# An attention and mixture-of-experts kernel: the first expert's load and making unpinned and in order of use, one cast two steps later

## The chip, the cores and the metric

The kernel runs on one core of a Trainium2 chip. The core has a matrix engine (TensorE, PE in the profile; its weight loads are shown apart as PEld), VectorE (DVE), ScalarE (ACT), GpSimd (POOL) and SyncE (SP), which here only issues DMAs. Each engine carries out its own instructions strictly in the order in which they stand in its queue, and waits for others by semaphores. Matmuls write to PSUM, everything else lies in SBUF, and 16 DMA engines move data between SBUF and the chip's memory. The metric is the time of one execution in microseconds; smaller is better.

## The reference

Clustered attention is followed by a mixture of eight experts. Batch B is 4, 8 heads, 768 tokens of 64 numbers; the experts see 3072 tokens of 512 numbers.

```python
mask = q_assign[:, :, :, None] == k_assign[:, :, None, :]
scores = np.where(mask, scale * q @ k.T, -1e9)
x = softmax(scores) @ v                      # (3072, 512) after reordering
P = np.exp(x @ w_gate - max)
for _ in range(8):                           # balance rows and columns
    P /= P.sum(1); P /= P.sum(0); P *= N / E
for e in range(8):
    h = np.maximum(x @ w1[e], 0.0)           # 512 -> 1024
    out += P[:, e:e + 1] * (h @ w2[e])       # 1024 -> 512
```

## The kernel before

**Two stages.** The attention stage is written as small processes (load a pair of heads, split it, chunk of exponentials, values, norms and so on) that a planner in the kernel, `Planner.run`, puts into one order by costs and due times. `Planner.keep_order` then pins that order: each new instruction gets a dependency, without a semaphore, on the instruction before it on its engine, so that the scheduler of the language, which would otherwise choose among what is ready, keeps it. The expert stage follows; its order is written out by hand, as generators that are advanced step by step, and `keep_order` is called after each step, so it is pinned too. `self.last` holds the last instruction of each engine and `self.traced` how many have been pinned; because both simply go on from attention to the experts, the first instruction of the expert stage on each engine is pinned behind the last one of attention on that engine, on SP too.

**An iteration.** The expert stage takes a batch b (768 tokens, `xs[b]`, seven combinations of its four quarters) and a piece of an expert: 256 of its 1024 hidden columns, four pieces an expert, numbered `idx`. `layer1` forms the hidden block from seven products of quarter blocks in place of eight (the names A11 to S4 are the seven combinations of the weights' quarters, B11 to T4 those of x). Every operand is a high and a low float16 part, so a product is three matmuls on each of two column blocks. The seven products, each followed by a `yield`, are the seven steps m = 0 to 6 of an iteration; their order of use is A11, S2, A12, S3, S1, A22, S4. They use two PSUM banks (`h_ps`). `layer2` multiplies by the second matrix and runs one iteration later, one token tile a step (`before`). At each step other work is advanced beside it: the balancing of the gates (`gates`, L1023 to L1052, on DVE with small matmuls on PE), the scan of the next expert's weights for its largest value (`scan`, L286), the loading, maximum and splitting of the next batch's x (`next_x`, loads at L1152, maxima at L286, splits at L300 and L303), and the making of the next piece (`making`).

**Making a piece.** `load_raw` brings a piece of w1 (`r1`) and of w2 (`r2`) by the DMAs at L1074 and L1078. The raw tiles are two, used in turn (`wp0`, `wp1`). `make_w` scales both (L1087, L1098), forms the four sums S1 to S4 (L1096), casts the seven blocks to a high float16 part on ACT (L1101, L1104) and subtracts it for the low part (L1102, L1105), into the tile `wa`; then it does the same with w2 into `wb` (L1107, L1108). The casts are on ACT, the sums and subtractions on POOL, but for piece 0, which is made by DVE, all at once, ahead of the loop over the iterations. In the loop one part of the making is done in each of the steps m = 0 to 4, the cast and subtraction of `wb` in the fifth. In the iterations of an even batch (b = 0) the made piece is stored to memory (`store_w`, L1113 and L1114, on SP at the iteration's start), whence the other batches load it.

**Memory.** Attention's tile pools are closed when it ends, and the expert stage's pools are placed in the same part of SBUF in the order of the code. An instruction that writes to an expert tile therefore waits until those attention tiles are no longer read that lay there.

**Around the change.** After `plan.run()` the code goes `load_raw(0)`, `load_raw(1)`, `make_w(0, wt, nc.vector)` to its end, and then the loop. The first iteration puts on SP the store of piece 0, `load_raw(2)`, two scan tiles and the four quarters of batch 1's x. Just before all of these, the end of attention has the last store of x (`xd<-xT`, L918), which waits for the last multiplication of attention's output by its row factors (L909). The logits for the gates come from the same x (L935 to L951).

Of the kernel before, what the change touches and what calls it, by code (L numbers as in the profile page):

```python
# [13 lines left out]
AF = mybir.ActivationFunctionType  # L14
ALU = mybir.AluOpType
# [5 lines left out]
P = 128  # L21
# [37 lines left out]
class Planner:  # L59
# [16 lines left out]
    def keep_order(self):  # L76

        for i in self.instructions()[self.traced :]:
            if i.engine in self.last:
                info = mybir.DependencyInfo(mybir.DependencyClass.NoSync, mybir.DependencyReason.DATA)  # L80
                self.tc.add_manual_dep(i, self.last[i.engine], info, reason="planned order")
            self.last[i.engine] = i.name
        self.traced = len(self.instructions())

    def copied(self, time):

        self.queues = max(self.queues, self.now.time + 0.55) + time
        return self.queues + 1.4
# [64 lines left out]
def attn_moe_kernel(  # L153
# [11 lines left out]
    nc = tc.nc  # L165
# [50 lines left out]
    KC = NC // 2  # L216
# [10 lines left out]
    s1 = const.tile([P, E], F32, name="s1")  # L227
    s2 = const.tile([P, E], F32, name="s2")
# [79 lines left out]
    with ExitStack() as actx:  # L308
# [104 lines left out]
        plan = Planner(tc)  # L413
# [641 lines left out]
    A22, A11, A12, S1, S2, S3, S4 = range(7)  # L1055

    def w_tiles(made):

        pool = wq0 if made else wq1
        wa = pool.tile([P, 2, 7, KC, P], F16, name="wa", bufs=3 if made else 2)  # L1060
        wb = pool.tile([P, 2, 2, DO], F16, name="wb")
        return wa, wb
# [4 lines left out]
    raws = {}  # L1067
# [13 lines left out]
    def make_w(idx, wt, by=nc.gpsimd):  # L1081

        e = idx // NP2
        r1, r2 = raws.pop(idx)
        wa, wb = wt
        raw = r1[:, 0 : 4 * KC * P]
        nc.scalar.activation(raw, raw, AF.Copy, scale=s1[:, e : e + 1])  # L1087
        A = raw.rearrange("p (k c t f) -> p t k c f", k=2, c=KC, t=2)
        S_ = r1[:, 4 * KC * P :].rearrange("p (o c f) -> p o c f", o=4, c=KC)
        for o, a, b_, op in (  # L1090
            (0, A[:, 0, 0], A[:, 0, 1], ALU.add),
            (1, S_[:, 0], A[:, 1, 0], ALU.subtract),
            (2, A[:, 1, 0], A[:, 0, 0], ALU.subtract),
            (3, A[:, 1, 1], S_[:, 1], ALU.subtract),
        ):
            by.tensor_tensor(out=S_[:, o], in0=a, in1=b_, op=op)  # L1096
        yield
        nc.scalar.activation(r2, r2, AF.Copy, scale=s2[:, e : e + 1])  # L1098
        yield
        for o, a in ((A22, A[:, 0, 1]), (slice(A11, A12 + 1), A[:, 1])):  # L1100
            nc.scalar.copy(wa[:, 0, o], a)  # L1101
            by.tensor_tensor(out=wa[:, 1, o], in0=a, in1=wa[:, 0, o], op=ALU.subtract)  # L1102
        yield
        nc.scalar.copy(wa[:, 0, 3:7], S_)  # L1104
        by.tensor_tensor(out=wa[:, 1, 3:7], in0=S_, in1=wa[:, 0, 3:7], op=ALU.subtract)  # L1105
        yield
        nc.scalar.copy(wb[:, 0], r2)  # L1107
        by.tensor_tensor(out=wb[:, 1], in0=r2, in1=wb[:, 0], op=ALU.subtract)  # L1108
        yield

    def store_w(idx, wt):
        fa, fb = flat(*wt)
        nc.sync.dma_start(out=wd[idx][:, 0:W1C], in_=fa)  # L1113
        nc.sync.dma_start(out=wd[idx][:, W1C:], in_=fb)  # L1114
# [185 lines left out]
    load_raw(0)  # L1300
    load_raw(1)
    wt = made[0] = w_tiles(True)
    for _ in make_w(0, wt, nc.vector):
        pass
    t = 0
    for n, (b, e) in enumerate(order):
        if e == 0:
# [4 lines left out]
        for f2 in range(NP2):  # L1312
# [5 lines left out]
            if t in begins:  # L1318
                i = begins[t]
                made[i] = w_tiles(True)  # L1320
                making = make_w(i, made[i])
                if i + 1 < NI:
                    load_raw(i + 1)
# [33 lines left out]
            if nb is not None:  # L1357
                wt = made.pop(nidx) if nb == 0 else wn
# [27 lines left out]
```

## Time and profile before

| what | value |
|---|---|
| median of 3 runs | 2471.73 us (2467.83 to 2471.76) |
| the profiled execution | 2472.1 us, span 2470.3 us |
| PE busy | 2380.3 us, 96% of the span |
| DVE, ACT, POOL busy | 1360.9, 834.8 and 668.6 us |
| DMA | 320.29 MB, mean 130 GB/s |
| mean granted PE clock | 0.990 of full speed |

Times in the profile are counted from the start of the span. A row of the timeline gives start, duration, engine, line, operation, output and inputs; in brackets the idle time of the engine before it and what ended it. SPq is SP's queue of DMA issues: its rows show when a DMA is issued, not when the data have landed. A row of the waits gives who waited for whom, the total, the number of times and the longest. Rows that gather a line's instructions give the shortest, median and longest duration in ns and the first and last start.

### The profile page before, as it was taken

How to read it: one execution, taken by the hardware profiler on the slowest of the kernel's cores; microseconds unless marked ns; L12 is line 12 of the kernel's file. 1: busy time of each engine (PE TensorE's matmuls, PEld its weight loads, DVE VectorE, ACT ScalarE, POOL GpSimd, SP SyncE). 2: the span in 40 equal slices, each digit the busy share in tenths (PEclk: the TensorE clock that was granted, in tenths of full speed). 3: DMA queues.
4: the chain of work that ended last, by engine and by line, in shares of the span. 5: the costliest groups of instructions: out<-in, count | busy, mean ns of one | idle time of the engine just before them, and what ended most of it. 6: DMA issues, size and time to landing. Idle time of an engine off the chain costs nothing.

```text
span 2470.3 us, 32700 instructions
## 1 busy us (share of the span) xinstructions
PE 2380.3 (96%) x12848; PEld 1274.8 (52%) x12848; DVE 1360.9 (55%) x2372; ACT 834.8 (34%) x1608; POOL 668.6 (27%) x712
## 2 busy tenths in 40 slices
PE   7999999966999999999999999999999999999999
PEld 4555655533545555555555555555555555555554
DVE  7888888847555454545454445544444444444444
ACT  4555555543243333333333323222121222122121
POOL 5776777734053333222222221000000000000000
PEclk9999999988999999999999999999999999999999
DMA  6545465243356353536352334222322222222322
GB/s 145 117 104 117 106 151 137 72 171 134 122 212 240 148 185 139 198 128 218 114 211 105 134 133 157 95 94 95 113 98 94 94 106 106 94 95 99 113 103 90
DMA packets 154681, 320.29 MB, mean 130 GB/s; under 512 B 61088, under 2 KB 90528, under 8 KB 154016
## 3 DMA queue, kind: packets, MB, share of 16 engines
q1 hardware_dynamic: 154528, 318.21, 39.2%
q8 instruction: 101, 1.65, 0.3%
q14 instruction: 52, 0.43, 0.1%
HBM read 230.74 MB, written 58.72 MB: 117 GB/s over the span
## 4 chain that ended last, share of the span: by engine, by line
PE 87%; DVE 8%; ACT 2%; DMA 1%; issue 1%; POOL 1%; SPq 0%; ACTq 0%; DVEq 0%; POOLq 0%
PE h_ps L1181 34%; PE o_ps L1251 13%; PE o_ps L1249 13%; PE o_ps L1250 13%; PE av_ps L820 4%; PE max_ps L693 3%; PE exp_ps L761 2%; PE exp_ps L762 2%; DVE mrt L697 2%; DVE hl L1197 1%; PE misc_ps L553 1%; DVE vsum L503 1%; POOL psum L787 0%; DVE am L286 0%; ACT pe L768 0%
## 5 line engine op out<-in xcount | busy, mean ns | idle before, releaser
L1181 PEld LDWEIGHTS <-wa 128*128 128x128 f16 x5376 | 527.0, 98 | 454.5 <-issue 22.0
L1181 PE MATMUL h_ps<-xsT,wa 128*128 128x384 f16 x3072 | 584.7, 327 | 9.5 <-DVE gm L240 4.8
L1251 PE MATMUL o_ps<-wb,hl 128*128 128x512 f16 x1536 | 584.4, 380 | 8.9 <-DVE hl L1197 8.9
L1197 DVE SCALAR_TENSOR_TENSOR hl<-c,hh 128x384 f16<-128x384 f32 x512 | 312.0, 609 | 509.5 <-ACT hh L1194 509.3
L1250 PE MATMUL o_ps<-wb,hh 128*128 128x512 f16 x1536 | 584.4, 380 | 0.0
L1249 PE MATMUL o_ps<-wb,hh 128*128 128x512 f16 x1536 | 584.3, 380 | 0.0
L1194 ACT ACTIVATE hh<-c 128x384 f16<-128x384 f32 x512 | 267.6, 523 | 921.8 <-DVE c L1209 914.2
L1181 PE MATMUL h_ps<-xsB,wa 128*128 128x384 f16 x2304 | 420.8, 328 | 10.8 <-ACT wa L1101 7.1
L1251 PEld LDWEIGHTS <-hl 128*128 128x128 f16 x1536 | 150.5, 98 | 194.5 <-DVE hl L1197 13.3
L1209 DVE SCALAR_TENSOR_TENSOR c<-h_ps,u 128x384 f32<-128x384 f32 x256 | 142.0, 555 | 180.2 <-PE h_ps L1181 180.2
L1209 DVE SCALAR_TENSOR_TENSOR u<-h_ps,m 128x384 f32<-128x384 f32 x256 | 142.4, 556 | 171.8 <-PE h_ps L1181 171.4
L787 POOL TENSOR_TENSOR psum<-psum,pe 128x512 f32<-128x512 f32 (+1 forms) x203 | 221.6, 1109 | 48.3 <-ACT pe L768 41.8
L1096 POOL TENSOR_TENSOR r<-r 128x256 f32<-128x256 f32 x124 | 88.7, 736 | 511.7 <-ACT r L1087 509.3
L1249 PEld LDWEIGHTS <-hh 128*128 128x128 f16 x1536 | 151.1, 98 | 139.5 <-issue 1.0
L1250 PEld LDWEIGHTS <-hh 128*128 128x128 f16 x1536 | 150.3, 98 | 139.8 <-issue 1.0
L1214 ACT ACTIVATE c<-h_ps 128x384 f32<-128x384 f32 x128 | 62.7, 490 | 440.5 <-PE h_ps L1181 440.5
L697 DVE TENSOR_REDUCE mrt<-max_ps 128x1 f32<-128x512 f32 (+1 forms) x288 | 190.0, 683 | 37.0 <-PE max_ps L693 35.0
L768 ACT ACTIVATE pe<-exp_ps 128x512 f32<-128x512 f32 x288 | 165.6, 597 | 84.3 <-PE exp_ps L762 78.1
L1269 DVE SCALAR_TENSOR_TENSOR acc<-o_ps,gates,acc 128x512 f32<-128x512 f32 x168 | 125.4, 747 | 40.4 <-PE o_ps L1251 40.3
L820 PE MATMUL av_ps<-pe,vn 128*64 128x512 f32 (+1 forms) x768 | 136.3, 498 | 0.0
L693 PE MATMUL max_ps<-kX,qX 96*128 96x256 f32 (+1 forms) x384 | 126.8, 393 | 6.9 <-DVE mrt L697 4.2
L762 PE MATMUL exp_ps<-qX,kX 98*128 98x512 f32 (+1 forms) x384 | 127.9, 346 | 0.0
(199 smaller groups left out, 1915.0 us busy)
## 6 DMA issues: line engine op xcount, KB each, us to landing
wa<-wd SPq DMA_DIRECT2D x96, 896.0 KB
wb<-wd SPq DMA_DIRECT2D x96, 512.0 KB
r<-in_moe_w SPq DMA_DIRECT2D x64, 512.0 KB
wd<-wa SPq DMA_DIRECT2D x32, 896.0 KB
scan<-in_moe_w SPq DMA_DIRECT2D x56, 512.0 KB
wd<-wb SPq DMA_DIRECT2D x32, 512.0 KB
qn<-in_q SPq DMA_DIRECT2D x16, 384.0 KB
kn<-in_k SPq DMA_DIRECT2D x16, 384.0 KB
```

The costliest lines, as they stand in the source:

```text
L693: nc.tensor.matmul(ps[:, y * (z - a) : (y + 1) * (z - a)], t["qa"][0:96, i * P : (i + 1) * P], t["k2"][0:96, a:z], start=True, stop=True)
L697: nc.vector.tensor_reduce(out=t["mr"][:, i0 : i0 + ni, ni - 1], in_=ps.rearrange("p (x c) -> p x c", x=ni), axis=AX, op=ALU.max)
L762: nc.tensor.matmul(o, t["k2"][0:98, ki], t["qa"][0:98, a:z], start=False, stop=True)
L787: (nc.gpsimd if e == POOL else nc.vector).tensor_tensor(out=st[:, a:z], in0=old[a], in1=part, op=ALU.add)
L820: nc.tensor.matmul(av[o, a:z], vn[:, i, :], heads[t]["pe", c][:, i - i0], start=(i == 0), stop=False, skip_group_check=True)
L1181: nc.tensor.matmul(ps[:, 0:HB], wa[:, w_, a, c, :], x[:, x_, c, :], start=(first and s_ == 0), stop=(s_ == len(steps) - 1), skip_group_che ...
L1194: nc.scalar.activation(hh[:, 2 - i, o], src, AF.Relu)
L1197: nc.vector.scalar_tensor_tensor(out=hl[:, 2 - i, o], in0=src, scalar=0.0, in1=hh[:, 2 - i, o], op0=ALU.max, op1=ALU.subtract)
L1209: nc.vector.scalar_tensor_tensor(out=t, in0=ps[:, 0:HB], scalar=KAPPA, in1=x, op0=ALU.mult, op1=ALU.add)
L1249: nc.tensor.matmul(po[i], hh[:, t, ti], wbh[:, t], start=(first and t == 0), stop=False)
L1250: nc.tensor.matmul(po[i], hh[:, t, ti], wbl[:, t], start=False, stop=False)
L1251: nc.tensor.matmul(po[i], hl[:, t, ti], wbh[:, t], start=False, stop=(last and t == 1))
```

## The change

Three things. The planner gets `unpin`, which forgets the last instruction of each engine and counts everything issued so far as dealt with. It is called after the first piece's loads and making; so these instructions are pinned to nothing, and the chain of the expert stage begins anew with the first iteration, pinned within itself and not behind attention. The first piece is made by `make_first` in place of `make_w`: the same arithmetic on ACT and DVE, but with each part cast and subtracted as soon as its inputs are there, in the order A11 and A12, S1 and S2, S3 and S4, A22, then the second matrix. The cast of S1 to S4 in one instruction becomes two. In `make_w`, which makes all other pieces, two empty steps are put ahead of the second matrix's cast and subtraction, so that they come in the seventh step of an iteration and not in the fifth.

```diff
@@ class Planner
+    def unpin(self):
+
+        self.last, self.traced = {}, len(self.instructions())
@@ def make_w
         nc.scalar.copy(wa[:, 0, 3:7], S_)
         by.tensor_tensor(out=wa[:, 1, 3:7], in0=S_, in1=wa[:, 0, 3:7], op=ALU.subtract)
         yield
+        yield
+        yield
         nc.scalar.copy(wb[:, 0], r2)
         by.tensor_tensor(out=wb[:, 1], in0=r2, in1=wb[:, 0], op=ALU.subtract)
         yield
+
+    def make_first(wt):
+
+        r1, r2 = raws.pop(0)
+        wa, wb = wt
+        raw = r1[:, 0 : 4 * KC * P]
+        A = raw.rearrange("p (k c t f) -> p t k c f", k=2, c=KC, t=2)
+        S_ = r1[:, 4 * KC * P :].rearrange("p (o c f) -> p o c f", o=4, c=KC)
+
+        def parts(o, a):
+            nc.scalar.copy(wa[:, 0, o], a)
+            nc.vector.tensor_tensor(out=wa[:, 1, o], in0=a, in1=wa[:, 0, o], op=ALU.subtract)
+
+        def sum_(o, a, b_, op):
+            nc.vector.tensor_tensor(out=S_[:, o], in0=a, in1=b_, op=op)
+
+        nc.scalar.activation(raw, raw, AF.Copy, scale=s1[:, 0:1])
+        parts(slice(A11, A12 + 1), A[:, 1])
+        sum_(0, A[:, 0, 0], A[:, 0, 1], ALU.add)
+        sum_(1, S_[:, 0], A[:, 1, 0], ALU.subtract)
+        parts(slice(S1, S2 + 1), S_[:, 0:2])
+        sum_(2, A[:, 1, 0], A[:, 0, 0], ALU.subtract)
+        sum_(3, A[:, 1, 1], S_[:, 1], ALU.subtract)
+        parts(slice(S3, S4 + 1), S_[:, 2:4])
+        parts(A22, A[:, 0, 1])
+        nc.scalar.activation(r2, r2, AF.Copy, scale=s2[:, 0:1])
+        nc.scalar.copy(wb[:, 0], r2)
+        nc.vector.tensor_tensor(out=wb[:, 1], in0=r2, in1=wb[:, 0], op=ALU.subtract)
@@ after plan.run()
     wt = made[0] = w_tiles(True)
-    for _ in make_w(0, wt, nc.vector):
-        pass
+    make_first(wt)
+
+    plan.unpin()
     t = 0
```

## The prediction

> **What bounds the kernel now.** I read the slices of the span first, then stretches around the weak slices, then SP's queue in order of time, then the waits there.
>
> ```profile
> PE   7999999966999999999999999999999999999999
> DMA  6545465243356353536352334222322222222322
> ```
>
> One slice is 61.8 us. PE is full except in slices 8 and 9 (494 to 618 us), where attention ends and the experts begin. The stretches put numbers on it; columns are length, busy time and count of PE, PEld, DVE, ACT and POOL, granted clock, DMA share, GB/s.
>
> ```profile
> 520.00:628.00 108.00, 69.28 (x327) 34.06 (x328) 71.24 (x147) 37.07 (x55) 35.91 (x28) 0.82 0.54 189
> 628.00:2470.30 1842.30, 1824.32 (x9734) 950.62 (x9731) 862.00 (x1493) 512.91 (x927) 264.70 (x232) 1.00 0.36 131
> 489.00:520.00 31.00, 27.00 (x152) 13.93 (x152) 14.11 (x19) 14.51 (x34) 17.46 (x20) 0.96 0.00 1
> 524.70:531.77 7.07, 0.00 (x1) 0.01 (x1) 2.18 (x7) 3.17 (x5) 0.00 (x0) 0.72 0.97 322
> 541.00:550.20 9.20, 0.02 (x1) 0.00 (x0) 2.44 (x4) 1.46 (x3) 1.68 (x2) 0.71 1.03 370
> ```
>
> After 628 us PE has 18 us idle in 1842: nothing the change does there can win or lose much. From 520 to 628 it is idle 38.7 us, and 16.3 of these are two holes: 524.70 to 531.77, after attention's last matmul, and 541 to 550. In both the DMA engines are full (0.97, 1.03), while in the 31 us before 520 they move nothing (0.00). Work for DMA comes in one heap. SP's queue shows why (start, us, engine, line; the last row is from the list of SP's waits: in total, times, longest):
>
> ```profile
> 487.81 1.38 SPq L741 DMA_DIRECT2D nht<-mt  x2
> 520.42 0.34 SPq L918 DMA_DIRECT2D xd<-xT  x1
> 520.87 0.38 SPq L1074 DMA_DIRECT2D r<-in_moe_w  x1
> ...
> 533.95 0.34 SPq L1113 DMA_DIRECT2D wd<-wa  x1
> ...
> 539.51 2.34 SPq L1152 DMA_DIRECT2D xqB<-xd  x4
> SPq L918 <- DVE xT L909: 31.1, 1, 31.1
> ```
>
> SP stands 31.1 us behind the last store of x, which waits for attention's last multiplication; both experts' loads are pinned behind it. And who waits for these transfers:
>
> ```profile
> ACT r L1087 <- DMA r<-in_moe_w: 9.8, 1, 9.8
> DVE am L286 <- DMA xqB<-xd: 8.3, 1, 8.3
> 531.77 2.10 PE L1181 MATMUL h_ps<-xsB,wa 128*128 128x384 f16 x6 [7.07 <-ACT wa L1101]
> 534.97 0.35 DVE L1025 TENSOR_REDUCE gmax<-lg 128x1 f32<-128x192 f32 x1
> 538.58 0.27 DVE L1030 TENSOR_REDUCE g<-h_ps 1x1 f32<-1x128 f32 x1
> 547.13 0.95 DVE L286 TENSOR_REDUCE am<-xqB 128x1 f32<-128x768 f32 x1 [8.28 <-DMA xqB<-xd]
> ```
>
> The first hole is expert 0's first load and its making. The second is the maximum over batch 1's first quarter of x: it sits in DVE's hand-ordered queue ahead of the additions that free PE's banks, and its load is the last of SP's heap. These are the only two long waits for a DMA between 500 and 625; from 547 to 628 engines wait for each other. So a maximum that can run earlier carries all behind it along, up to the PE-bound part.
>
> **The first load and making, freed.** Four DMAs (L1074 and L1078 twice) and the making lose their place behind attention's last steps; the experts' own order after them stays pinned within itself, but no longer behind attention. What then holds each one is its memory. By the pools' sizes, added up in the order of the code, expert piece 0's raw buffer takes the place of the q and k inputs, read last by L589 at 446.1: it can land while DMA is idle. The made tile lies on kL0, kL2, qX0, which the last exp matmuls read, and raw piece 1 on the row sums, which L857 reads:
>
> ```profile
> L589 PE MATMUL misc_ps<-qn,cm x8: 486/498/510, 411.1 to 446.1; 128*32 128x384 f32 x8
> 510.73 0.28 PE L762 MATMUL exp_ps<-qX,kX 98*128 98x256 f32 x1
> 514.22 0.85 PE L857 MATMUL misc_ps<-psum,ones 128*32 128x384 f32 x8
> 518.68 0.80 PE L904 MATMUL misc_ps<-rt,spread 36*128 36x128 bf16 x6 [0.35 <-ACT rt L896]
> 524.74 0.21 DVE L951 COPY lg<-misc_ps 128x48 f32<-128x48 f32 x1 [0.48 <-PE misc_ps L947]
> 530.80 0.91 ACT L1101 CAST wa<-r 128x256 f16<-128x256 f32 x2
> 531.62 1.04 ACT L1104 CAST wa<-r 128x1024 f16<-128x1024 f32 x1
> 533.83 1.22 DVE L1108 TENSOR_TENSOR wb<-r,wb 128x1024 f16<-128x1024 f32 x1
> ```
>
> So making can write from 511, and loads of piece 1 can go from 515.1, where the first load's 520.87 stands now. The making left after 511 is ACT's casts, 0.91 + 1.04 + 1.04 = 3 us and 0.2 for one cast split in two, and the subtractions beside it, the last 1.22: over by about 516 to 518 with attention's own small steps between. ACT is busy 14.51 of the last 31 us, DVE 14.11: room enough. The order of use itself (A11 first) is worth nothing then, as pieces are made before they are asked for. If that cover fails and making starts late, it is worth the 0.3 to 1.5 us by which A11 comes ahead of A22 and the sums.
>
> What is late next? The pinned chain's first DVE step needs the gates' logits (L951, 524.95). PE can run three products before it, and DVE comes to the maximum 3.6 us after it (534.97 to 538.58 now), at 528.6. A freed instruction in front of attention's last chain can hold it: nothing, or a cast's 1 us at three links; that moves 528.6 to 531.6 at most. So the load of x decides. Ahead of it in SP's queue stand, in their old order, the store of made piece 0 (896 + 512 KB, 1.44 MB, by the tiles' shapes), raw piece 2 (1.05), two scan tiles (1.05), then x's first quarter (0.39): 3.93 MB. At the rate of the second hole, 370 GB/s, these take 10.6 us; from 533.95 that gives 544.6, and the maximum began at 547.13, so 2.5 us go to start and landing. After the change raw piece 1 (1.05) starts at about 516, the others follow without a gap, and the last store of x (1.57 MB) is ready at 520.4, likely before the scans, as it has the older place: 6.55 MB, 17.7 us, 516 + 17.7 + 2.5 = 536.2, **10.9 us earlier**. With that store behind x's load it is 4.98 MB, 13.5 us, 532.0: 15.1 earlier. If raw piece 1 must wait for the whole attention pool (L904 reads of it until 519.5), 520 + 17.7 + 2.5 = 540.2: 6.9 earlier. I take 10.9, since each buffer, not the pool, is what is read, and keep 6.9 and 15.1. The issue itself does not limit: SP needs about 7 us for the list, from 516 to 523. Early loads cost attention nothing I can see; bounded by 0 and 1 us.
>
> **The second matrix's cast, two steps later.** Cast and subtraction of wb move from the fifth to the seventh step of an iteration, the store behind them on SP too. The relu rows are those of the seventh step, behind which the cast now stands.
>
> ```profile
> 549.01 1.03 ACT L1107 CAST wb<-r 128x1024 f16<-128x1024 f32 x1
> 555.36 0.53 ACT L1194 ACTIVATE hh<-c 128x384 f16<-128x384 f32 x1 [3.87 <-DVE c L1209]
> 573.53 1.03 ACT L1107 CAST wb<-r 128x1024 f16<-128x1024 f32 x1
> 581.69 0.52 ACT L1194 ACTIVATE hh<-c 128x384 f16<-128x384 f32 x1 [4.21 <-DVE c L1209]
> 584.43 1.14 ACT L1087 ACTIVATE r<-r,s 128x1024 f32<-128x1024 f32 x1
> ...
> L1042 DVE TENSOR_TENSOR pr<-pr,rsum x8: 357/358/1886, 552.6 to 616.1; 128x192 f32<-128x192 f32 x8
> 566.17 2.11 POOL L1105 TENSOR_TENSOR wa<-r,wa 128x1024 f16<-128x1024 f32 x1
> 566.61 1.89 DVE L1042 TENSOR_TENSOR pr<-pr,rsum 128x192 f32<-128x192 f32 x1
> 602.42 2.12 POOL L1108 TENSOR_TENSOR wb<-r,wb 128x1024 f16<-128x1024 f32 x1 [6.17 <-ACT wb L1107]
> 604.60 1.92 DVE L1052 TENSOR_TENSOR pr<-pr,csum 128x192 f32<-128x192 f32 x1
> ```
>
> On SP the first two stores move by 6 to 8 us (549 to 556, 574 to 582), and the loads of raw pieces 3 and 4 behind them. Piece 3 is read first at 584.43, some 20 us after it would then land: hidden. The tile is multiplied an iteration later. Past 628 PE's full queue hides it. What is not hidden is POOL's 2.12 us subtraction: it moves to about 557, 583 and 613, where DVE runs the gates' steps (552.6 to 616.1 in its row), on which PE waits. The gates' multiplication L1042 (shortest, median, longest of eight: 357, 358, 1886 ns) took 1.89 us where POOL subtracted beside it. So a meeting costs 1.5; three cost 4.6. The third stood among such steps already (604.60 took 1.92), which gives up to 1.6 back; POOL's and ACT's next work is pushed by 1 to 3 us, now into other DVE steps, now out of them. Bounds: 1.6 gained to 4.6 lost; I take **2.5 lost**, the first two meetings (3.0) less a part of what the third gives back.
>
> The Trainium skill (SBUF — State Buffer, Who interferes with whom) says that VectorE with two SBUF inputs and a GpSimd instruction that reads SBUF share a port pair as an exclusive lock, whoever is second being blocked to the other's end. By that rule, which the rows at 566 and 604 bear out, three meetings could cost up to three whole subtractions, 6.4 us, and the sum below would be 2467.6; the rule speaks against this half of the change.
>
> **Sum:** 2472.1 (the profiled execution; span 2470.3, 1.8 outside it) - 10.9 + 2.5 = 2463.7. That execution stands 0.4 over the median of the runs, 2471.73, no more than they scatter.
>
> **Rivals.**
> 1. *The store of x goes behind.* The maximum starts at 532.0, and no meeting with POOL to 2.5 lost: 2472.1 - 15.1 + 0 to 2.5, about 2458. For it: the list is short and SP free. Against: the store is ready at 520.4, before the scans' places are. DVE's 528.6 caps it at 18.5 earlier.
> 2. *Another wait takes the place.* Buffers come free late, the heap stays one heap: -6.9 + 2.5 to 4: about 2468. For: every pool of the experts lies on a pool of attention, in use up to 520.
> 3. *The unpinned loads come where they were.* If the compiled order leaves them behind the store, only A11's lead (0.3 to 1.5) and the meetings remain: about 2473. Against: SP has nothing else for 31 us.
> 4. *Slower: POOL's moved subtraction on the gates' chain.* The place is DVE between 553 and 616; the price up to one subtraction, 2.12, a meeting, 6.4 for three: 2478.5 if the loads win nothing. It decides as soon as x comes less than about 6 us sooner, for instance because a freed load or scaling stands waiting in a queue in front of attention's last steps.
>
> **How the numbers follow.** Forecast 0.52, its own range 2459 to 2467; rival 1 0.17, rival 2 0.12, rival 3 0.09, rival 4 0.10. The range, 2455 to 2470.5, holds the forecast, most of rivals 1 and 2, and leaves out the rest of 1, and 3 and 4. A measurement tells about 0.2% (5 us) from nothing: faster takes the forecast nearly whole (0.50), rival 1 and a little of 2, 0.69; the same, the remainder of these and rival 3, 0.20; slower rival 4 and a bit of 3, 0.11.
>
> **What would show it.** Right: two DMAs of r between 460 and 511 and two at 515 to 518 on SP; the first L1181 before 525; one hole left on PE, ending with the maximum (L286 from xqB) at 536 give or take 4; from there to the PE-bound part some 80 us as before, plus 1 to 4. Wrong: r still issued at 521; the maximum within 5 us of 547; a freed step of the experts waiting in front of attention's; gates' steps at 2 us in new places; PE with less than 1824 of 1842 us after the start.

## The result, and the profile after

| | before | after |
|---|---|---|
| median of 6 runs | 2471.6 us (2467.83 to 2471.76) | 2455.32 us (2451.57 to 2455.81) |
| profiled execution, its span | 2472.1, 2470.3 us | 2455.3, 2453.5 us |
| ratio of the times | | 0.9935, 95% interval 0.9922 to 0.9947 |

The change makes the kernel 16.3 us faster. The forecast was 8 us, to 2463.7, and the range 2455 to 2470.5: the sign was right, the size half of what came, and the median lies just inside the lower end.

SP's queue of the changed kernel around the end of attention (start, us, line; some rows between are left out). The loads of raw pieces 0 and 1, the two stores of piece 0 and the load of x are the rows to look for:

```profile
460.74 0.38 SPq L1078 DMA_DIRECT2D r<-in_moe_w  x1
461.18 0.50 SPq L1082 DMA_DIRECT2D r<-in_moe_w  x1
513.89 0.35 SPq L1147 DMA_DIRECT2D wd<-wa  x1
515.00 0.35 SPq L1148 DMA_DIRECT2D wd<-wb  x1
515.40 1.06 SPq L1078 DMA_DIRECT2D r<-in_moe_w  x1
518.95 0.32 SPq L922 DMA_DIRECT2D xd<-xT  x1
519.37 0.38 SPq L1078 DMA_DIRECT2D r<-in_moe_w  x1
519.81 2.46 SPq L1082 DMA_DIRECT2D r<-in_moe_w  x2
525.40 0.34 SPq L283 DMA_DIRECT2D scan<-in_moe_w  x1
527.02 2.01 SPq L1186 DMA_DIRECT2D xqB<-xd  x4
```

Raw piece 0 is issued at 460.74, long before attention ends, where it was issued at 520.87. Piece 0 is made and stored at 513.89, ahead of the last store of x (518.95), where the store came 13.5 us behind it. The load at 515.40 is raw piece 2; piece 1 is the one at 519.37. So the transfers are the same, but the list that begins with piece 0's stores begins 20 us sooner, ahead of the last store of x. From 520 to 535 us the DMA engines are full in each stretch of 5 us (shares 1.00, 1.05 and 1.06): the heap is still there, only earlier. The timeline of the engines shows what that was worth:

```profile
512.89 1.15 PE L1215 MATMUL h_ps<-xsB,wa 128*128 128x384 f16 x6
521.55 0.21 DVE L955 COPY lg<-misc_ps 128x48 f32<-128x48 f32 x1 [0.48 <-PE misc_ps L951]
527.88 1.15 ACT L1091 ACTIVATE r<-r,s 128x1024 f32<-128x1024 f32 x1 [10.72 <-DMA r<-in_moe_w]
530.74 0.37 PE L1032 MATMUL h_ps<-ident,gmax 128*1 128x128 f32 x1 [6.94 <-ACT c L1248]
534.21 0.95 DVE L290 TENSOR_REDUCE am<-xqB 128x1 f32<-128x768 f32 x1 [1.08 <-DMA xqB<-xd]
615.66 2.11 PE L1215 MATMUL h_ps<-xsB,wa 128*128 128x384 f16 x12
```

The first product runs at 512.89, between attention's last matmuls, in place of 531.77. The maximum of x's first quarter, L290 here and L286 before, begins at 534.21 in place of 547.13, and its wait for the load has shrunk from 8.28 to 1.08 us. One hole on PE is left around attention's end, the 6.94 us ahead of 530.74, and it has a new cause: ACT stands 10.72 us before the scaling of raw piece 1, and the copy of c that frees PE's bank is queued behind it.

The last row is a landmark that every version has, and that I use below: the twelve matmuls with which the last product of the fourth iteration runs into the first of the fifth. Behind it PE is full, and I call it the start of the full part. Before the change it is this row:

```profile
626.54 2.11 PE L1181 MATMUL h_ps<-xsB,wa 128*128 128x384 f16 x12
```

Now the span can be split at two places, the issue of attention's last store of x, S (520.42 and 518.95), and this landmark (626.54 and 615.66):

| stretch | before | after | gain |
|---|---|---|---|
| to S (attention) | 520.42 | 518.95 | 1.47 |
| S to the maximum's begin | 26.71 | 15.26 | 11.45 |
| the maximum to the full part | 79.41 | 81.45 | -2.04 |
| the full part to the end | 1843.76 | 1837.84 | 5.92 |
| span | 2470.3 | 2453.5 | 16.8 |

The first is attention, whose instructions are in the same order in both. In the kernel before and the four experiments that keep the loads pinned, where nothing ahead of S differs, S lies anywhere between 516.96 and 524.29 us, so 1.47 can't be told from chance, and the experiments are read from S. The last row of the parts is the surprise: 5.9 us in the part that was full before.

### The profile page after: what moved, and what is told of

The parts are those of the page before. It is cut to its first block, busy times and chain, and to the rows that moved or that the text cites. A ratio compares the mean times of both kernels' runs of the same rounds, so it can differ in the third digit from the quotient of the medians.

```text
span 2453.5 us, 32700 instructions
## 1 busy us (share of the span) xinstructions
PE 2380.3 (97%) x12848; PEld 1275.8 (52%) x12848; DVE 1343.6 (55%) x2373; ACT 834.6 (34%) x1609; POOL 668.9 (27%) x712
## 4 chain that ended last, share of the span: by engine, by line
PE 87%; DVE 8%; DMA 2%; issue 1%; ACT 1%; POOL 1%; SPq 0%; ACTq 0%; POOLq 0%; DVEq 0%
PE h_ps L1215 34%; PE o_ps L1285 13%; PE o_ps L1283 13%; PE o_ps L1284 13%; PE av_ps L824 4%; PE max_ps L697 2%; PE exp_ps L765 2%; DVE mrt L701 2%; PE exp_ps L766 2%; DVE vsum L507 1%; PE misc_ps L557 1%; DMA scan<-in_moe_w 1%; POOL psum L791 0%; DVE hl L1231 0%; PE misc_ps L861 0%
## 5 line engine op out<-in xcount | busy, mean ns | idle before, releaser
L1231 DVE SCALAR_TENSOR_TENSOR hl<-c,hh 128x384 f16<-128x384 f32 x512 | 291.0, 568 | 507.6 <-ACT hh L1228 507.3
```

Source lines behind the costliest of these rows:

```text
L1231: nc.vector.scalar_tensor_tensor(out=hl[:, 2 - i, o], in0=src, scalar=0.0, in1=hh[:, 2 - i, o], op0=ALU.max, op1=ALU.subtract)
```

## The experiments

My theory before the runs was that there are two gains: the loads' at attention's end, and the later cast's in the full part. The rivals were that the loads made all of it, and that chance in attention made much of it. The first four kernels take the change apart.

**The loads alone.** The new steps in `make_w` are left out.

```diff
-        yield
-        yield
         nc.scalar.copy(wb[:, 0], r2)
```

> The freed first loads and first making without the later cast. Theory (two gains): x's load ends the wait some 12 to 13 us sooner as in the changed kernel, and the part behind it keeps its 9 us of PE waiting for hl: 10 to 12 us under the kernel before, 2460 to 2462. Rival (the loads alone made it all): about 16 us, 2455. Rival (chance in attention): under 9 us.

Measured: 2460.61 us, ratio 0.9955 (0.9943 to 0.9968), 11 us faster.

**The cast alone.** The kernel before with these two steps added.

> The later cast and subtraction of the second matrix alone. Theory (two gains): PE's waits for hl in the PE-bound part go from 8.9 us to under 1, some 6 to 7 us won there, about 2 lost among the gates' steps: 2466 to 2468. Rival (the loads alone made it all): no change or 2 to 3 us more, 2471 to 2474, with the waits for hl as they were or as chance has it.

Measured: 2464.58 us, ratio 0.9973 (0.9962 to 0.9984), 6.7 us faster. Neither half is the whole, and 0.45 and 0.27 per cent add up to the 0.65 of the change within the intervals. PE's waits of the full part in the loads' version and in the cast's version (total us, times, longest):

```profile
PE o_ps L1283 <- DVE hl L1229: 8.9, 9, 1.4
```

```profile
PE o_ps L1253 <- DVE hl L1199: 0.4, 2, 0.2
```

The wait for hl stays as it was, 8.9 us, with the loads alone and is gone with the cast alone. Measured from S, the landmarks say the same for both:

| version | S | to the maximum | to the full part | full part to the end |
|---|---|---|---|---|
| before | 520.42 | 26.71 | 106.12 | 1843.76 |
| loads alone | 520.91 | 15.67 | 97.23 | 1843.76 |
| cast alone | 516.96 | 26.76 | 107.79 | 1837.75 |
| both (the change) | 518.95 | 15.26 | 96.71 | 1837.84 |

```profile
520.91 0.32 SPq L922 DMA_DIRECT2D xd<-xT  x1
536.58 0.95 DVE L290 TENSOR_REDUCE am<-xqB 128x1 f32<-128x768 f32 x1 [1.24 <-DMA xqB<-xd]
618.14 2.11 PE L1213 MATMUL h_ps<-xsB,wa 128*128 128x384 f16 x12
```

```profile
516.96 0.35 SPq L918 DMA_DIRECT2D xd<-xT  x1
543.72 0.95 DVE L286 TENSOR_REDUCE am<-xqB 128x1 f32<-128x768 f32 x1 [8.34 <-DMA xqB<-xd]
624.75 2.11 PE L1183 MATMUL h_ps<-xsB,wa 128*128 128x384 f16 x12
```

The loads win 11.0 us up to the maximum and 8.9 up to the full part, and nothing in it. The cast's version is 1.7 us longer up to the full part and wins 6.0 in it. The rivals fall. The full part is the firmest of these numbers: over all thirteen profiles it takes 1843.6 to 1843.9 us in the five that leave the cast in the fifth step and 1835.4 to 1837.9 in the eight that move it. The stretch from the maximum to the full part is the loosest: 78.2 to 81.6 us with the cast in the fifth step, 78.8 to 83.0 with it later.

**Unpinned, but made in the old order.** `make_w(0, wt, nc.vector)` stands in place of `make_first(wt)`, `plan.unpin()` stays, the later cast is left out.

> The freed first loads, with the first piece made in the old order (A22 first, sums first) and no later cast. Theory: the order of making is worth next to nothing, since the piece is made before PE asks for it: within 2 us of the kernel with freed loads and the new order. Rival (order of use carries a part): 3 us or more above that one.

Measured: 2459.99 us, ratio 0.9952 (0.9939 to 0.9965), as fast as the loads with the new order. In its profile the maximum begins 16.23 us behind S and the full part 94.70, against 15.67 and 97.23.

**Made in the new order, but pinned.** `make_first(wt)` without `plan.unpin()`, the later cast left out.

> The new order of making with the loads pinned behind attention as before, and no later cast. Theory: A11 is ready 0.3 to 1.5 us sooner, but the load of x, the last in SP's list, still ends the second wait at about 547 us: 0 to 1 us faster, 2470 to 2472. Rival (order of use carries a part): 3 us or more faster.

Measured: 2473.45 us, ratio 1.0013 (1.0003 to 1.0023): no gain, rather a loss of 3 us, which neither theory nor rival had. ACT's queue in this version, and DVE's last subtraction:

```profile
532.25 1.15 ACT L1130 ACTIVATE r<-r,s 128x1024 f32<-128x1024 f32 x1 [9.56 <-DMA r<-in_moe_w]
533.43 0.62 ACT L1124 CAST wa<-r 128x512 f16<-128x512 f32 x1
535.60 0.62 ACT L1124 CAST wa<-r 128x512 f16<-128x512 f32 x1 [1.55 <-DVE r L1128]
537.65 0.92 ACT L1124 CAST wa<-r 128x512 f16<-128x512 f32 x2 [1.43 <-DVE r L1128]
...
540.73 1.22 DVE L1141 TENSOR_TENSOR wb<-r,wb 128x1024 f16<-128x1024 f32 x1 [1.41 <-ACT wb L1140]
```

With casts and sums in turns, ACT waits 1.55 and 1.43 us for DVE's sums, and from the scaling's begin to the last subtraction's end the making takes 9.7 us (532.25 to 541.95), where the old order took 6.6 (528.43 to 535.05). Both stores and the list behind them come later. On the path the order of use is dear; unpinned it is hidden, as the run before shows. So the gain at attention's end is the unpinning's alone.

**Why the later cast wins in the full part.** I had priced it by POOL's subtraction, which can hold up DVE. Here is one of the places where PE waited for hl before the change, in order of time by engine:

```profile
956.47 1.04 ACT L1107 CAST wb<-r 128x1024 f16<-128x1024 f32 x1 [2.45 <-PE o_ps L1251]
957.42 0.52 ACT L1194 ACTIVATE hh<-c 128x384 f16<-128x384 f32 x1
957.59 2.12 POOL L1108 TENSOR_TENSOR wb<-r,wb 128x1024 f16<-128x1024 f32 x1 [4.22 <-ACT wb L1107]
957.97 2.16 DVE L1197 SCALAR_TENSOR_TENSOR hl<-c,hh 128x384 f16<-128x384 f32 x1 [2.24 <-ACT hh L1194]
960.19 0.39 PE L1251 MATMUL o_ps<-wb,hl 128*128 128x512 f16 x1 [1.37 <-DVE hl L1197]
...
ACT wb L1107 <- PE o_ps L1251: 14.7, 6, 2.5
```

Two things meet there. The cast to wb waits 2.45 us on ACT for PE, because its buffer is still read by the last matmuls of the second layer, and the relu behind it in ACT's queue (957.42) is late by that; then hl, which needs the relu, runs beside POOL's subtraction and takes 2.16 in place of 0.56 us. Six of PE's nine waits for hl are of this kind, 1.37 us each and 8.2 of the 8.9 us. Which of the two makes PE wait? The first kernel for it moves the subtraction and leaves the cast.

```diff
         nc.scalar.copy(wb[:, 0], r2)
+        yield
+        yield
         by.tensor_tensor(out=wb[:, 1], in0=r2, in1=wb[:, 0], op=ALU.subtract)
```

> The kernel before, with the second matrix's subtraction on POOL two steps later and its cast on ACT left in the fifth step. Theory (POOL's subtraction holds up DVE's hl): PE's waits for hl fall from 8.9 us to under 1 as with cast and subtraction moved, the part behind the start is 6 us shorter: 2465 to 2468. Rival (the cast on ACT stands in front of hh, and so of hl): 8.9 us as before, 2470 to 2473.

Measured: 2469.03 us, ratio 0.9983 (0.9971 to 0.9995), and in the waits:

```profile
PE o_ps L1253 <- DVE hl L1199: 8.9, 9, 1.4
ACT wb L1107 <- PE o_ps L1253: 14.7, 6, 2.5
```

The 8.9 us are untouched, and so is the full part, 1843.85 us. The time itself lies between the two forecasts, some 4 us faster than before; in the profile 1.2 us of it lie between S and the full part and 3.2 ahead of S, where nothing was changed. But that alone does not clear POOL: nothing stands on POOL between the two places, so the subtraction can still run as soon as the cast is done, at the same moment as before. So this kernel did not test POOL's part. The next kernel moves the cast behind that relu, and no further.

```diff
+        yield
         nc.scalar.copy(wb[:, 0], r2)
         by.tensor_tensor(out=wb[:, 1], in0=r2, in1=wb[:, 0], op=ALU.subtract)
```

> The kernel before, with the second matrix's cast and subtraction one step later, not two. Theory (the cast waits on ACT for the buffer of wb, which the last matmuls of the second layer still read, and the relu of the sixth step stands behind it): behind that relu the cast runs at the same moment as before and hurts nobody: hl waits under 1 us, 6 us won behind the start, 2464 to 2468. Rival (POOL's subtraction itself blocks hl, whenever it runs then): it runs at the same moment as before, so most of the 8.9 us stay, 2469 to 2473.

Measured: 2465.03 us, ratio 0.9972 (0.9961 to 0.9983), as much as with two steps. The groups of this version (busy us, mean ns, then idle time before them) and its waits:

```profile
L1252 PE MATMUL o_ps<-wb,hl 128*128 128x512 f16 x1536 | 584.2, 380 | 0.4 <-DVE hl L1198 0.4
L1198 DVE SCALAR_TENSOR_TENSOR hl<-c,hh 128x384 f16<-128x384 f32 x512 | 309.8, 605 | 498.5 <-ACT hh L1195 498.2
```

```profile
PE o_ps L1252 <- DVE hl L1198: 0.4, 2, 0.2
ACT wb L1108 <- PE o_ps L1252: 1.1, 6, 0.2
```

PE's wait is gone (0.4), while hl still takes 605 ns in the mean, against 609 before and 568 in the changed kernel; 32 of the 512 take over 1 us, against 29 before and 7 in the changed kernel. So DVE is held beside POOL here as often as before, and it does not matter: the hl that is held is one that comes in time. What brings the loss about is one place in ACT's queue, the cast that waits for a buffer ahead of a relu that does not. In the place shown above POOL's subtraction takes part in it: started at 957.97 and with its 0.56 us, hl would have ended at 958.53, before PE began to wait for it at 958.82. The cast's place lets the two meet at that hl; with the cast one step later the subtraction runs behind it. Whether a subtraction held back by itself would do as well, no run shows.

The move has a price of its own, which keeps it from winning all 8.5 us. Some 75 us into the full part PE waits for c once, 1.5 to 2.7 us in the eight profiles with the cast moved and 1.3 to 1.5 in the five without; and right behind this wait the granted clock is 0.50 for 3.4 or 6.8 us in all eight (from 692.4 to 699.2 in the changed kernel) and 1.00 in all five. One step wins 8.4 us in the full part of its profile, two steps 6.0; the times, 0.9972 and 0.9973, do not tell the two apart.

**What binds now.** The changed profile has two loads that end late together, piece 1's and x's. One kernel issues the load of the next x, the four DMAs of `next_x` for batch 1, ahead of the unpinning, so that it is free as well (`load_x` holds these DMAs, and `next_x` calls it for the later batches alone):

```diff
     make_first(wt)
+    load_x(1)
 
     plan.unpin()
```

> The changed kernel, with the load of batch 1's x issued ahead of the unpinned chain, so that it can run while DMA is idle. Theory (two loads arrive together: x's maximum waits 1.1 us for x, but the step in front of it waits for piece 1's raw load): 1 to 2 us under the changed kernel, 2453 to 2454.5, with piece 1's scaling on ACT still at about 528. Rival (x's load alone decides): 5 us or more, under 2450.5.

Measured: 2456.98 us, ratio 0.9935 (0.9918 to 0.9952): nothing won, where theory and rival both had a gain.

```profile
533.10 1.15 ACT L1091 ACTIVATE r<-r,s 128x1024 f32<-128x1024 f32 x1 [10.49 <-DMA r<-in_moe_w]
539.20 0.93 DVE L290 TENSOR_REDUCE am<-xqB 128x1 f32<-128x768 f32 x1
```

The maximum no longer waits for x, but S is 524.39 in this run, and it begins 14.81 us behind it, against 15.26: ACT still stands for piece 1.

Another places raw piece 1's pool `wp1` behind `wp0`, and `cp` behind `wq0`. In the changed kernel's trace the load waits for a semaphore each of ACT, POOL and PE, whose last updates before it are those of attention's row factors (L900 to 517.2, L893 to 516.4, L908 to 517.9), and it stands on SP behind the last store of x (518.95). By the prediction's working of the places, its own bytes held the row sums, which were read last at 512.95 (L861). So it seems that a pool of attention is given back as a whole; the run tests the place alone.

```diff
     wp0 = ...
-    cp = ...
+    wp1 = ...
     wq0 = ...
+    cp = ...
     wq1 = ...
     hp = ...
-    wp1 = ...
```

> The changed kernel, with raw piece 1's buffer placed where the pool of attention is done at the last exp matmul and not at attention's last row factors. Theory (that pool held the load until 519 us): the load goes before the last store of x, PE's 6.9 us wait for c is gone, x's load lands some 3 us sooner: 2 to 4 us under the changed kernel, 2451 to 2453.5. Rival (the place makes no difference): 2454.5 to 2456.

Measured: 2452.23 us, ratio 0.9916 (0.9899 to 0.9932): the number lies in the theory's range, but the interval overlaps the changed kernel's, so a gain is not shown. From S to the full part the profile has 96.04 us, against 96.71.

```profile
510.04 0.38 SPq L1078 DMA_DIRECT2D r<-in_moe_w  x1
533.67 0.95 DVE L290 TENSOR_REDUCE am<-xqB 128x1 f32<-128x768 f32 x1 [6.30 <-DMA xqB<-xd]
```

Piece 1 is loaded at 510, ACT and PE do not wait for it, and now the maximum waits 6.30 us for x. It begins 13.81 us behind S (519.86): 1.5 sooner, not 3. Each alone leaves the other's wait. Together:

> The two above together. Theory (with both loads out of the way DVE reaches the maximum 3.6 us after the logits): the maximum begins about 8 us sooner against the last store of x than in the changed kernel, and the kernel is 5 to 9 us faster, 2446 to 2450. Rival (the gates' steps and POOL bind behind it anyway): 0 to 3 us, 2452 to 2455.

Measured: 2445.18 us, ratio 0.9889 (0.9874 to 0.9903), wholly below the changed kernel's interval: 0.46 per cent, some 11 us, faster than it and a little more than the theory had.

```profile
516.54 0.32 SPq L922 DMA_DIRECT2D xd<-xT  x1
523.70 0.93 DVE L290 TENSOR_REDUCE am<-xqB 128x1 f32<-128x768 f32 x1
602.52 2.11 PE L1220 MATMUL h_ps<-xsB,wa 128*128 128x384 f16 x12
```

The maximum begins 7.16 us behind S, 8.1 sooner than in the changed kernel, without a wait, and the full part 10.7 sooner (85.98 behind S). S itself, 516.54, is 2.4 us sooner here, by chance as far as is known.

Two more vary this version. With piece 0 made in the old order:

> Both early loads and the later cast, with piece 0 made in the old order. Theory (the order of making is worth nothing once the loads are early): within 2 us of the one in the order of use, 2443 to 2447. Rival (the order of use counts): 3 us or more slower.

Measured: 2448.24 us (2440.3 to 2450.55), ratio 0.9898 (0.9879 to 0.9918). The median is 3 us more, at the rival's edge, but the interval is as wide as that and the full part begins 86.02 us behind S, as with the new order: no difference that these runs can show. With the cast one step later and not two:

> Both early loads and the order of use, with the cast one step later and not two. Theory: the same 6 us behind the start, and a subtraction that meets the gates' steps elsewhere: within 2 us of the one with two steps, 2443 to 2447. Rival (the place among the gates' steps decides): 3 us or more to either side.

Measured: 2444.86 us, ratio 0.9889 (0.9876 to 0.9903): the same. In its profile the full part begins 88.69 us behind S, 2.7 later than with two steps, which the times do not bear out. These two and the version above are the best that were found.

## Why the prediction was right, and where its size was off

- **The loads and what binds at attention's end: right.** The path was read as SP's list, then x's load, then the maximum. The term was 10.9 us, the maximum expected at 536.2; it came at 534.21, 12.9 sooner, 11.45 of it behind S. In the two versions with the loads alone the same term is 11.0 and 10.5. Two parts of the way there were otherwise: the list starts with the store of piece 0 (513.89) and not with the load of piece 1 at 516, so that start came out near by luck; and SP's issue, said not to limit, stands 3.0 us ahead of the scan's loads until the store of x has landed (525.34), which costs little, as the DMA engines stay full.
- **The order of use, worth nothing: right**, as far as it is hidden. The aside that it might be worth 0.3 to 1.5 us if making were late is wrong: pinned, it makes the making 3.1 us longer.
- **Raw piece 1 from 515.1, rival 2's mechanism set aside: wrong, and not costly to the sum.** I took it that the load is free once its buffer's last reader is done. It waited for later steps, and went at 519.37. Piece 0's stores and piece 2 filled the time, so the list did not start later; but piece 1, being late, put a new wait on ACT and PE (10.72 and 6.94 us), which the prediction did not have, and so the one hole left on PE does not end with the maximum. It lies almost wholly under the wait for x, as the run with x's load alone freed shows.
- **The later cast between the maximum and the full part, 2.5 us lost: near in number, by luck as far as these runs show.** That stretch is 2.04 us longer in the change and 1.6 with the cast alone, but with the loads alone, where the cast stays, it is 2.15 longer too. So in the change the later cast adds no loss to that of the loads' version: the full part begins 96.71 us behind S with it and 97.23 without. And a sooner maximum does not carry all behind it along exactly: with the loads alone the 11.0 us at the maximum become 8.9 at the full part, and in the other such version 10.5 become 11.4. The foretold meetings do occur: the first row of DVE below is held beside the moved subtraction of wb, and so are two more, at 574.2 and 602.2 (1.64 and 1.67 us); the second row meets the subtraction of wa, which was not moved. No run took the meetings away, and what lengthens the stretch stays open. One row was misread in the prediction, too: 604.60 stood beside the combining of x on POOL (L296, 604.50 to 606.30), not beside the subtraction of wb, which had ended at 604.54.

```profile
544.43 2.06 DVE L1055 TENSOR_SCALAR csum<-csum 128x8 f32<-128x8 f32 x1
555.22 2.23 DVE L1056 TENSOR_TENSOR pr<-pr,csum 128x192 f32<-128x192 f32 x1
544.33 2.13 POOL L1114 TENSOR_TENSOR wb<-r,wb 128x1024 f16<-128x1024 f32 x1 [8.13 <-ACT wb L1113]
555.12 2.12 POOL L1109 TENSOR_TENSOR wa<-r,wa 128x1024 f16<-128x1024 f32 x1
```

- **The step that failed: "Past 628 PE's full queue hides it."** In the full part I priced the cast at nothing, because PE had 18 us idle in 1842. Half of that idle time had one cause, and the page of the profile named it: PE idle 8.9 us before the matmuls with hl, ended by DVE's hl. I read it as remains and not as a term. The cast's move shortens the full part by 5.9 us, 70 per cent of the 8.4 us by which the forecast was too small; attention's chance, 1.5, and half a microsecond each at the maximum and behind it are the rest. The missing question was what stood ahead of hl's relu on ACT, and what that waited for.
- Rival 1's time of about 2458 would have been nearer, but by another way: x's store did not go behind.

## What to carry to other kernels

A small share of idle time in an otherwise full stretch is still a sum worth reading: ask of each repeated wait which instruction stands ahead of the late one in its engine's queue, and on whose buffer. An instruction that must wait for a buffer goes behind those that need not; here one step was enough. When loads are freed, look at what their memory waits for, and expect several loads to be late together: freeing one of them alone can win nothing, as here, while both together won another 11 us.

## What the runs showed of the hardware

In the changed kernel, with the experts' first products between attention's last matmuls, PE's granted clock did not fall there. The 24 matmuls for the logits, before and after, and the stretches around them (length, then busy time and count of PE, PEld, DVE, ACT, POOL, clock, DMA share, GB/s):

```profile
520.12 3.64 PE L935 MATMUL misc_ps<-xT,wg 128*32 128x256 f32 x24 [0.64 <-DVE xT L909]
520.10:523.80 3.70, 3.64 (x24) 1.34 (x24) 0.29 (x1) 0.00 (x0) 0.00 (x0) 0.50 0.76 299
```

```profile
518.64 1.93 PE L939 MATMUL misc_ps<-xT,wg 128*32 128x256 f32 x24 [0.74 <-DVE xT L913]
518.00:521.60 3.60, 2.31 (x26) 1.13 (x27) 1.39 (x4) 0.00 (x0) 0.00 (x0) 1.00 1.07 380
```

They took 3.64 us at a clock of 0.50 and 1.93 at 1.00, though nothing in them was changed. The logits follow S by 4.3 us before (524.74) and by 2.6 after (521.55). But the products alone do not keep the clock up. This is the same row with the loads unpinned and the old order of making:

```profile
521.51 3.50 PE L939 MATMUL misc_ps<-xT,wg 128*32 128x256 f32 x24 [0.47 <-DVE xT L913]
```

Of the eight versions with products there, four have these matmuls at a clock of 1.00, in 1.93 us, and four at 0.53 to 0.59, in 3.2 to 3.5 us; the five without are all at 0.50 to 0.52, in 3.6 us.

The time of attention itself varies: over the thirteen profiles S lies between 516.5 and 524.4 us with attention's own order untouched. The clock goes with it. The profiles show only two values of it, 0.50 and 1.00, and a value between is a mean of the two. In the profile of before, the stretch from 230 to 270 us ran at a mean of 0.91, because the clock was 0.50 from 241.0 to 247.9, and in the changed kernel's at 1.00. In the five profiles with 0.91 there S lies between 520.4 and 524.4, in the eight with 1.00 between 516.5 and 520.9. Why it falls in one run and not in another stays open.
